# Filling the array's rows and columns in the logits, the first tiles and the expert layers of an mLSTM and mixture-of-experts kernel

## The chip, the cores and the metric

The kernel runs on one core of a Trainium2 chip. The metric is the device time of one execution in microseconds, over three runs before the change. The core has a matrix engine (PE; its weight loads are shown apart as PEld), a vector engine (DVE), a scalar engine (ACT), a general engine (POOL), a queue that issues DMAs (SP), and 16 DMA engines. A product on PE has a stationary operand that is loaded into an array of 128 rows by 128 columns, and a moving operand that streams through it. "64*128 64x256" in the profile is a product whose stationary operand has 64 rows and 128 columns and whose moving operand has 64 rows and 256 columns. The granted clock is the share of full speed that the throttle gave PE.

## The reference, cut to what matters

A gated recurrence over 768 steps for 4 batches and 8 heads of 40 values makes 3072 rows x of 320 values. Each row goes to the one of 8 experts that has its largest logit; the expert has two layers, 320 to 1024 and back.

```python
for t in range(S):
    m_new = np.maximum(f_gate[:, :, t] + m, i_gate[:, :, t])
    ...
    C = f_stab * C + i_stab * np.einsum('bhd,bhe->bhde', vt, kt)
    n = f_stab * n + i_stab * kt
    y[:, :, t] = sigmoid(o_gate) * (C @ qt) / np.maximum(np.abs(n @ qt), 1.0)
logits = x @ w_gate
e_idx = np.argmax(logits, axis=1)
eom = 1.0 / (1.0 + np.exp(-(x @ w_output_gate)))
for e in range(E):
    mask = e_idx == e
    h = np.maximum(x[mask] @ w1[e], 0.0)
    out[mask] = gate_w[mask, None] * eom[mask, e, None] * (h @ w2[e])
```

## The kernel before

**First stage.** With these gates the state is settled after the first 64 steps. For each batch `causal` makes masked products of the first 64 steps (`Pm`), `state` makes the settled state (`Cm`), and `hats` multiplies the queries, which stand as columns in `qTt`, with them. A batch has six tiles of 128 tokens, done in pairs: 12 pairs in all, numbered n. In the first tile of a batch the first 64 tokens come from `Pm` (L958) and the other 64 from `Cm` (L964), so these products have 64 columns; `qTt` holds only the queries after the first 64 steps. DVE and POOL make rows of x from `hat` (L1072 to L1088). `logits_of` turns a tile of 128 rows to columns with three transposes (L1147: 128, 128 and 64 values), ACT copies them out in two pieces (L1135, L1137), and `logits` (L368) multiplies them with the 16 columns of `wg`: three products for a tile, the third with 64 rows. These are f32 products, and each is shown in the profile as two records. `route` finds the expert and the place of each row; its first product (L246) has a stationary operand of one row. `hots` and `place` (L347, result `tp`) turn places into tables of row numbers.

**The early expert.** The largest expert after the first batch has its first 256 rows done within this stage by `pair_products` (L679 first layer, L695 second layer), while the last tiles are still being routed.

**Expert layers.** Then all eight experts run in order of size with fixed capacities C (256 left of the early one, then 512, 472, 464, 384, 368, 344, 300). f32 numbers are split into a rounded part (h) and a rest (l). `expert_hidden` (L730) takes eight blocks of 128 hidden values; a block is eight products into one accumulator: for each of the first two 128 values of x, `w1h*xh`, `w1h*xl`, `w1l*xh`; for the last 64 values, which stand twice in `xh` (rows 0 to 63 rounded, rows 64 to 127 the rest), one product of 128 rows with `w1h` and one of 64 rows with `w1l`. ACT (L731) and DVE (L732) move the result out. `expert_rows` (L746) makes the output tiles; the next expert's weights are loaded, rounded by ACT (L566, L574) and their rest made by DVE (L567, L575) meanwhile.

**What sets the order.** From `manual_schedule` on, each engine's instructions stand in the order in which the program emits them. In the first stage the class `Play` emits the operations of several lines of work by estimated times; in the expert layers plain loops do it. `warmup` emits products of constants (L991) that nobody reads: nine at the start, some between, and more where `Play` expects PE to idle.

## Time and profile before

| what | value |
|---|---|
| three runs | 328.77, 340.69, 341.56 us; median 340.69 us |
| span of the profiled execution, first to last instruction | 350.8 us |
| PE / PEld / DVE / ACT / POOL busy in it | 332.7 / 284.0 / 168.8 / 135.0 / 95.1 us |
| mean granted clock of PE in it | 0.872 |
| first stage, up to the first product of the expert layers | about 119 us |

The page gives no time of the profiled execution beside its span, so the span stands for it; it is 10.1 us longer than the median and 9.2 us longer than the slowest of the three runs. The views of the profile used here are: the windows (for a stretch of time the busy time of each engine with the number of instructions, the granted clock PEclk, the busy share of the DMA engines and what they moved), the timeline (start and duration of each instruction, like neighbours merged as xN), and the groups by form (count, busy time, mean ns of one, idle time of the engine ahead of them and who ended it). The end of a product is modelled and products overlap; the distance from one start to the next is the better measure of what one costs.

### The profile page before, as it was taken

How to read it: one execution, taken by the hardware profiler on the slowest of the kernel's cores; microseconds unless marked ns; L12 is line 12 of the kernel's file. 1: busy time of each engine (PE TensorE's matmuls, PEld its weight loads, DVE VectorE, ACT ScalarE, POOL GpSimd, SP SyncE). 2: the span in 40 equal slices, each digit the busy share in tenths (PEclk: the TensorE clock that was granted, in tenths of full speed). 3: DMA queues.
4: the chain of work that ended last, by engine and by line, in shares of the span. 5: the costliest groups of instructions: out<-in, count | busy, mean ns of one | idle time of the engine just before them, and what ended most of it. 6: DMA issues, size and time to landing. Idle time of an engine off the chain costs nothing. (4 is left out here: it accounts for less than half of the span.)

```text
span 350.8 us, 5301 instructions
## 1 busy us (share of the span) xinstructions
PE 332.7 (95%) x1911; PEld 284.0 (81%) x1913; DVE 168.8 (48%) x446; ACT 135.0 (38%) x297; POOL 95.1 (27%) x121
## 2 busy tenths in 40 slices
PE   5989999999999999999999999999999999999960
PEld 2779899999868989768966996798798798798950
DVE  6671476563695527757045506712653744712100
ACT  3523144233332236556145515623543635612210
POOL 5170341244224321610360133023214124021020
PEclk9695587555556999999999999999999999999995
DMA  7997089332623675574336425351753753110010
GB/s 191 248 257 190 10 250 275 76 120 64 211 92 91 171 195 154 163 276 121 114 94 201 105 104 159 121 169 31 235 129 108 229 153 109 53 39 7 4 42 3
DMA packets 24370, 47.04 MB, mean 134 GB/s; under 512 B 2489, under 2 KB 17570, under 8 KB 24336
## 3 DMA queue, kind: packets, MB, share of 16 engines
q1 hardware_dynamic: 20976, 37.21, 37.6%
q0 software_dynamic: 3088, 9.15, 8.6%
q8 instruction: 17, 0.28, 0.3%
q10 hardware_dynamic: 272, 0.26, 0.3%
q14 instruction: 17, 0.14, 0.1%
HBM read 37.91 MB, written 9.06 MB: 134 GB/s over the span
## 5 line engine op out<-in xcount | busy, mean ns | idle before, releaser
L732 DVE SCALAR_TENSOR_TENSOR hl<-hp,hh 128x256 fp32r<-128x256 f32 (+7 forms) x64 | 35.9, 561 | 96.1 <-ACT hh L731 95.5
L730 PE MATMUL hp<-xh,w1l 128*128 128x256 f32 (+15 forms) x192 | 71.5, 373 | 0.0
L730 PE MATMUL hp<-xh,w1h 128*128 128x256 f32 (+7 forms) x192 | 70.9, 369 | 0.0
L746 PE MATMUL op<-w2h,hh 128*128 128x320 f32 (+4 forms) x208 | 64.9, 312 | 0.0
L746 PE MATMUL op<-w2l,hh 128*128 128x320 f32 (+4 forms) x208 | 64.2, 308 | 0.0
L746 PE MATMUL op<-w2h,hl 128*128 128x320 f32 (+4 forms) x208 | 64.1, 308 | 0.0
L750 POOL DMA_INDIRECT out<-ob,sro x24 | 24.3, 1014 | 144.9 <-ACT ob L749 127.1
L731 ACT ACTIVATE hh<-hp 128x256 fp32r<-128x256 f32 (+7 forms) x64 | 31.6, 494 | 56.9 <-PE hp L730 56.9
L730 PEld LDWEIGHTS hp<-xh,w1l 128*128 128x128 f32 (+1 forms) x192 | 35.7, 186 | 17.7 <-issue 15.1
L730 PEld LDWEIGHTS hp<-xh,w1h 128*128 128x128 f32 x192 | 36.0, 188 | 11.9 <-issue 5.9
L730 PE MATMUL hp<-xl,w1h 128*128 128x256 f32 (+7 forms) x128 | 43.4, 339 | 0.0
L749 ACT ACTIVATE ob<-op,xg 128x320 f32<-128x320 f32 (+4 forms) x26 | 13.7, 527 | 65.8 <-PE op L746 65.8
L746 PEld LDWEIGHTS op<-w2h,hh 128*128 128x128 f32 (+4 forms) x208 | 37.5, 180 | 0.4 <-issue 0.2
L746 PEld LDWEIGHTS op<-w2l,hh 128*128 128x128 f32 (+4 forms) x208 | 37.6, 181 | 0.2
L746 PEld LDWEIGHTS op<-w2h,hl 128*128 128x128 f32 (+4 forms) x208 | 37.5, 180 | 0.2
L368 PEld LDWEIGHTS gbank<-wg,xt 128*128 128x128 f32 x144 | 30.4, 283 | 2.1 <-ACT lg L1157 0.4
L368 PE MATMUL gbank<-wg,xt 128*128 128x16 f32 x144 | 31.3, 336 | 0.3 <-ACT lg L1157 0.3
L547 POOL DMA_INDIRECT xg<-xs,srg x24 | 26.2, 1093 | 14.3 <-DVE sr_z L431 7.3
L567 DVE TENSOR_TENSOR w1l<-ws,w1h 128x512 fp32r<-128x512 f32 x42 | 28.9, 688 | 2.2 <-ACT w1h L566 1.8
L575 DVE TENSOR_TENSOR w2l<-ws,w2h 128x640 fp32r<-128x640 f32 x28 | 22.9, 825 | 11.6 <-ACT w2h L574 11.0
L964 PE MATMUL hat<-Cm,qTt 120*128 120x123 f32 (+1 forms) x144 | 28.1, 368 | 0.0
L964 PEld LDWEIGHTS hat<-Cm,qTt 120*128 120x128 f32 (+1 forms) x144 | 25.8, 263 | 1.0 <-issue 0.8
(220 smaller groups left out, 439.0 us busy)
## 6 DMA issues: line engine op xcount, KB each, us to landing
ws<-in_w SPq DMA_DIRECT2D x16, 640.0 KB, 5.0
ws<-in_w SPq DMA_DIRECT2D x16, 512.0 KB, 3.6
ws<-in_w SPq DMA_DIRECT2D x16, 256.0 KB, 3.9
xs<-xr SPq DMA_DIRECT2D x3, 1164.0 KB, 5.6
ot<-in_on SPq DMA_DIRECT2D x3, 960.0 KB, 10.8
qTt<-in_qT SPq DMA_DIRECT2D x6, 330.0 KB, 9.5
xs<-xr SPq DMA_DIRECT2D x1, 776.0 KB, 4.1
qTt<-in_qT SPq DMA_DIRECT2D x3, 220.0 KB, 10.2
```

The source lines that it names most:

```text
L368: nc.tensor.matmul(lg_ps[:, j], xt[:rn, kk, j], wg[:rn, kk], start=(kk == 0), stop=(kk == 2))
L547: nc.gpsimd.indirect_dma_start(out=xg[:M, j, :], out_offset=None, in_=xs[0:rows, :], in_offset=bass.IndirectOffsetOnAxis(ap=gi_[:M, j : j ...
L567: nc.vector.tensor_tensor(w1l[:, kk, us], x["st1"][kk][:, us], w1h[:, kk, us].bitcast(F32), ALU.subtract)
L575: rest.tensor_tensor(w2l[:, us], x["st2"][u][:, vs], w2h[:, us].bitcast(F32), ALU.subtract)
L730: nc.tensor.matmul(hp, a, c, start=(i == 0), stop=(i == len(mm) - 1))
L731: nc.scalar.activation(hh[:, f], hp, AF.Relu)
L732: nc.vector.scalar_tensor_tensor(hl[:, f], hp, 0.0, hh[:, f].bitcast(F32), ALU.max, ALU.subtract)
L746: nc.tensor.matmul(op[:M], a, c, start=(i == 0), stop=(i == len(mm) - 1))
L749: nc.scalar.activation(ob[:M, j], op[:M], AF.Copy, scale=xg[:M, j, DM + 64 : DM + 65])
L750: nc.gpsimd.indirect_dma_start(out=out[:, :], out_offset=bass.IndirectOffsetOnAxis(ap=x["oi"][:M, j : j + 1], axis=0), in_=ob[:M, j, :], i ...
L964: nc.tensor.matmul(hat[p0:, j, cg], qTt[:K, g, t0 : t0 + P - p0], Cm[b][:K, cg], start=True, stop=True)
```

## The change

Six edits, all of which leave the result the same to rounding:

1. The last product of a hidden block takes all 128 rows of `w1l` and `xh`, in `expert_hidden` and in `pair_products`. Rows 64 to 127 add the product of both rests.
2. The third transpose of a tile takes values 192 to 319 in place of 256 to 319; the third slice of the logit weights has zeros for the 64 that come twice. ACT copies all three pieces at once.
3. The logit weights stand five times side by side (`wg`, made by POOL from `wg1`), so the moving operand has 80 columns; the first 16 of the result are read.
4. `qTt` has all 768 columns, the first 64 zero, and `Pm` has 128 columns, the last 64 zero; in the first tile of a batch the products with `Cm` and with `Pm` are added in one accumulator over all 128 columns. Both tiles are now two fixed buffers each.
5. The first product of `route` takes 128 rows, of which only the first is not zero.
6. The constants of `warmup` are read from `ones` with step 0; the tile `wide` and its memset are gone.

```diff
+KL = [0, 128, 192]
+REP = 5
...
-        nc.tensor.matmul(pr, ones[0:1, :], bump[0:1].unsqueeze(1).to_broadcast([1, n, E]), start=True, stop=False)
+        nc.tensor.matmul(pr, ones, bump.unsqueeze(1).to_broadcast(full), start=True, stop=False)
...
     def logits(xt, j, lg_ps):
-        for kk, (r0, rn) in enumerate(KW):
-            nc.tensor.matmul(lg_ps[:, j], xt[:rn, kk, j], wg[:rn, kk], start=(kk == 0), stop=(kk == 2))
+        for kk in range(3):
+            nc.tensor.matmul(lg_ps[:, j], xt[:, kk, j], wg[:, kk].rearrange("p r e -> p (r e)"), start=(kk == 0), stop=(kk == 2))
...
-            mm += [(w1h[:, 2, fs], xh[:, 2]), (w1l[0:64, 2, fs], xh[0:64, 2])]
+            mm += [(w1h[:, 2, fs], xh[:, 2]), (w1l[:, 2, fs], xh[:, 2])]
...
-        lg_ps = gbank[:, 0 : 4 * E].rearrange("p (c e) -> p c e", e=2 * E)
+        lg_ps = gbank[:, 0 : 4 * E * REP].rearrange("p (c e) -> p c e", c=2)
...
+        qts = [gp.tile([120, 3, S], F32, name=f"qTt{i}") for i in range(2)]
+        pms = [gp.tile([P, 4, P], F32, name=f"Pm{i}") for i in range(2)]
+        for i in range(2):
+            nc.vector.memset(qts[i][:, :, :L0], 0.0)
+            nc.vector.memset(pms[i][:, :, L0:], 0.0)
...
-        nc.sync.dma_start(wg, wgo)
+        nc.sync.dma_start(wg1[:, 0:2], wgo[:, 0:2])
+        nc.sync.dma_start(wg1[64:128, 2], wgo[0:64, 2])
...
-                if c == 0:
-                    for i in range(4):
-                        nc.tensor.matmul(hat[:L0, j, 2 * i : 2 * i + 2], Pm[b][:, i], vab[b % 2][:, i], start=True, stop=True)
-                p0 = L0 if c == 0 else 0
-                t0 = c * P + p0 - L0
...
-                    nc.tensor.matmul(hat[p0:, j, cg], qTt[:K, g, t0 : t0 + P - p0], Cm[b][:K, cg], start=True, stop=True)
+                    nc.tensor.matmul(
+                        hat[:, j, cg], qTt[:K, g, c * P : (c + 1) * P], Cm[b][:K, cg], start=(g == 0), stop=(c > 0 and g == 2)
+                    )
+                if c == 0:
+                    for i in range(4):
+                        nc.tensor.matmul(hat[:, j, 2 * i : 2 * i + 2], Pm[b][:, i], vab[b % 2][:, i], start=False, stop=(i == 3))
...
-        wide = gp.tile([P, 512], BF16, name="wide")
-        nc.vector.memset(wide, 1.0)
...
-                nc.tensor.matmul(gbank, ones, wide, start=True, stop=True)
+                nc.tensor.matmul(gbank, ones, ones[:, 0:1].to_broadcast([P, 512]), start=True, stop=True)
...
+            nc.gpsimd.tensor_copy(wg, wg1.unsqueeze(2).to_broadcast([P, 3, REP, 2 * E]))
...
-                    yield act(256)
-                    nc.scalar.copy(xt[:, 0:2, j], xt_ps[:, 0:2])
-                    yield act(P)
-                    nc.scalar.copy(xt[0:64, 2, j], xt_ps[0:64, 2])
+                    yield act(3 * P)
+                    nc.scalar.copy(xt[:, :, j], xt_ps)
...
-                    for kk, (r0, rn) in enumerate(KW):
-                        nc.tensor.transpose(xt_ps[:rn, kk], rows_[b][:, c0 + j, r0 : r0 + rn], ident)
+                    for kk, r0 in enumerate(KL):
+                        nc.tensor.transpose(xt_ps[:, kk], rows_[b][:, c0 + j, r0 : r0 + P], ident)
```

Since `Play` is told of one copy where there were two, it also emits some work at other places.

First, PE where the logits of the first batch end and the products of the second begin. The names are result, moving and stationary operand; the rows before:

```order
L368 MATMUL gbank<-wg,xt 128x16 x3
L1147 MATMUL xt_ps<-ident,xr 128x128 x2
L1147 MATMUL xt_ps<-ident,xr 64x128
L964 MATMUL hat<-Cm,qTt 128x123 x2
L964 MATMUL hat<-Cm,qTt 128x82
L964 MATMUL hat<-Cm,qTt 128x123 x2
L964 MATMUL hat<-Cm,qTt 128x82
L958 MATMUL hat<-vab_201,Pm 64x82 x4
L964 MATMUL hat<-Cm,qTt 64x123 x2
L964 MATMUL hat<-Cm,qTt 64x82
```

The same place now:

```order
L372 MATMUL gbank<-wg,xt 128x80 x3
L1155 MATMUL xt_ps<-ident,xr 128x128 x3
L970 MATMUL hat<-Cm,qTt_174 128x123 x2
L970 MATMUL hat<-Cm,qTt_174 128x82
L970 MATMUL hat<-Cm,qTt_174 128x123 x2
L970 MATMUL hat<-Cm,qTt_174 128x82
L970 MATMUL hat<-Cm,qTt_174 128x123 x2
L970 MATMUL hat<-Cm,qTt_174 128x82
L975 MATMUL hat<-vab_210,Pm_176 128x82 x4
```

The number of products stays; the shapes with 64 and with 16 are gone, and in the first tile the products with `Pm` stand behind those with `Cm`.

Second, PE at the end of the first stage, where the places of the last tiles (`tp`) and the early expert's first layer (`two`) meet. The last products of the second block of `two` before, and the first of `tp` behind them:

```order
L679 MATMUL two<-xh,w1h 128x256
L679 MATMUL two<-xl,w1h 128x256
L679 MATMUL two<-xh,w1l 128x256
L347 LDWEIGHTS OH_1207
L347 MATMUL tp<-R_1208,OH_1207 128x48
```

There now, the last of `tp` and the first of `two`:

```order
L352 LDWEIGHTS OH_1184
L352 MATMUL tp<-R_1185,OH_1184 128x48
L683 MATMUL two<-xh,w1h 128x256
L683 MATMUL two<-xl,w1h 128x256
L683 MATMUL two<-xh,w1l 128x256
```

Before, 14 products of `two` stood ahead of `tp`; now all of `tp` stands ahead of `two`.

Third, DVE at the same place, whose `R` is what `tp` needs and whose `xl` and `xh` (rows of the early expert as columns, rest and rounded) are what `two` needs. Before (`xl` stands eleven rows further up):

```order
L629 TENSOR_TENSOR xh<-two,xh 64x256
L312 TENSOR_TENSOR ad<-io_94,q 128x12
L285 RECIPROCAL sm_1165<-sm_1165 128x16
L320 TENSOR_TENSOR OH_1207<-ioP,lo 128x256
L320 TENSOR_TENSOR OH_1169<-ioP,lo 128x256
L328 TENSOR_TENSOR ad<-ad,val 128x12
L379 COPY cnt<-ct 128x8
L290 TENSOR_REDUCE ss<-sm_1165 128x2
L332 TENSOR_TENSOR R_1208<-O,ad 128x96
L332 TENSOR_TENSOR R_1170<-O,ad 128x192
```

Now:

```order
L631 TENSOR_TENSOR xl<-two,xh 128x512
L325 TENSOR_TENSOR OH_1184<-ioP,lo 128x256
L337 TENSOR_TENSOR R_1130<-O,ad 128x192
L333 TENSOR_TENSOR ad<-ad,val 128x12
L383 COPY cnt<-ct 128x8
L295 TENSOR_REDUCE ss<-sm_1148 128x2
L337 TENSOR_TENSOR R_1185<-O,ad 128x96
L633 TENSOR_TENSOR xh<-two,xh 64x256
```

The last step of `xh` has moved behind both `R`, where it stood far ahead of them.

## The prediction

> **What bounds the kernel.** I read the page first, then the windows by stage, then PE's timeline inside each stage. From the page:

> ```profile
> span 350.8 us, 5301 instructions
> PE 332.7 (95%) x1911; PEld 284.0 (81%) x1913; DVE 168.8 (48%) x446; ACT 135.0 (38%) x297; POOL 95.1 (27%) x121
> ```

> PE is busy for 95% of the span, so PE is the engine to follow. The windows by stage show at which clock (after each engine's busy time and instruction count come PEclk, the DMA share and GB/s):

> ```profile
> 26.00:46.00 20.00, 20.00 (x115) 17.97 (x115) 7.05 (x30) 5.44 (x16) 4.14 (x8) 0.50 0.47 120
> 46.00:56.00 10.00, 10.00 (x94) 9.25 (x91) 8.51 (x37) 4.29 (x15) 3.54 (x8) 0.99 0.84 254
> 56.00:94.00 38.00, 37.73 (x196) 35.79 (x195) 19.66 (x82) 13.21 (x45) 13.18 (x13) 0.51 0.44 130
> 94.00:111.00 17.00, 16.21 (x84) 12.18 (x85) 13.13 (x55) 5.74 (x15) 6.18 (x5) 0.50 0.32 112
> 119.00:335.00 216.00, 216.00 (x1217) 183.24 (x1216) 98.40 (x166) 93.11 (x184) 52.61 (x50) 1.00 0.44 129
> ```

> The expert layers (119 to 335 us) are bound by PE at full clock: 216 of 216 us, DVE 98, ACT 93. The first stage is bound by PE too, but for 75 us (26 to 46 and 56 to 111) at a clock of 0.50. From 46 to 56 us the same kind of work ran at 0.99, with 94 records of products in 10 us against 115 in 20. The expert layers' blocks, at 128x256 and at 128x512 (start, duration):

> ```profile
> 127.52 0.39 PE L730 MATMUL hp<-xh,w1h 128*128 128x256 f32 x1
> 127.75 0.28 PE L730 MATMUL hp<-xl,w1h 128*128 128x256 f32 x1
> 128.34 0.28 PE L730 MATMUL hp<-xh,w1h 128*128 128x256 f32 x1
> 128.55 0.38 PE L730 MATMUL hp<-xh,w1l 64*128 64x256 f32 x1
> 128.86 0.39 PE L730 MATMUL hp<-xh,w1h 128*128 128x256 f32 x1
> ...
> 147.02 0.50 PE L730 MATMUL hp<-xh,w1h 128*128 128x512 f32 x1
> 147.35 0.39 PE L730 MATMUL hp<-xl,w1h 128*128 128x512 f32 x1
> 148.51 0.40 PE L730 MATMUL hp<-xh,w1h 128*128 128x512 f32 x1
> 148.84 0.50 PE L730 MATMUL hp<-xh,w1l 64*128 64x512 f32 x1
> 149.27 0.50 PE L730 MATMUL hp<-xh,w1h 128*128 128x512 f32 x1
> ```

> Between like products of 128 rows the starts are (128.34 - 127.75) / 5 = 0.118 us apart at 256 columns, and (148.51 - 147.35) / 5 = 0.232 at 512. Around the 64-row product the steps are 0.21, 0.31 and 0.23 us, then 0.33, 0.43 and 0.33. The weight loads say the same:

> ```profile
> L730 PEld LDWEIGHTS hp<-xh,w1l 64*128 64x128 f32 x64 | 11.7, 183 | 16.2 <-issue 15.1
> L730 PEld LDWEIGHTS hp<-xl,w1h 128*128 128x128 f32 x128 | 24.1, 188 | 0.8
> ```

> (The second row's columns are those of the first: busy, mean ns, idle ahead.) Ahead of the 64 loads with 64 rows PEld stood idle for 16.2 us with nothing to wait for; ahead of 128 loads with 128 rows, 0.8. [...]

> **The change, part by part.** *The hidden blocks (edit 1).* Eight equal steps would make 8 x 0.118 = 0.94 us where a block takes 128.86 - 127.52 = 1.34, and 1.86 where it takes 149.27 - 147.02 = 2.25: 0.40 and 0.39 us saved at either width. With 64 blocks, 25.2 us. What could take some back is DVE: at 256 columns, beside the weights' rest, a block needs the two rows below, 0.42 + 0.69 = 1.11 us, more than the new 0.94, but only in the first expert's last four blocks: 4 x 0.17 = 0.7. Wider blocks leave DVE room.

> ```profile
> 132.06 0.42 DVE L732 SCALAR_TENSOR_TENSOR hl<-hp,hh 128x256 fp32r<-128x256 f32 x1
> 132.56 0.69 DVE L567 TENSOR_TENSOR w1l<-ws,w1h 128x512 fp32r<-128x512 f32 x1
> ```

> Weight loads are the next suspect when PE is faster; the busy share of DMA was 0.44 there and would be about 0.44 x 216 / 191 = 0.50. So -24.5 us, between -21 (a few blocks that wait) and -25.2.

> *The early expert (edit 1) and its new place.* At half clock:

> ```profile
> 107.28 0.58 PE L679 MATMUL two<-xh,w1h 128*128 128x256 f32 x1
> 107.66 0.41 PE L679 MATMUL two<-xl,w1h 128*128 128x256 f32 x1
> 108.73 0.41 PE L679 MATMUL two<-xh,w1h 128*128 128x256 f32 x1
> 109.58 0.58 PE L679 MATMUL two<-xh,w1h 128*128 128x256 f32 x1
> ...
> 103.03 0.52 DVE L332 TENSOR_TENSOR R<-O,ad 128x96 f16<-128x96 bf16 x2
> ```

> A block takes 2.30 us where eight steps of (108.73 - 107.66) / 5 = 0.214 make 1.71: 0.59 each, 4.7 for eight at half clock, 3.2 at full. But the order now puts all of `tp` and both `R` ahead of these blocks. `R` ended at 103.55; the first block began at 99.75 (row below). That wait of up to 3.8 us is new, and what is queued behind it on PE is the whole early expert and then the expert layers. Together I take -0.5, between -4.7 (DVE's chain is early enough) and +0.6.

> ```profile
> 99.75 0.78 PE L679 MATMUL two<-xh,w1h 128*128 128x256 f32 x1
> ```

> *Logits (edits 2 and 3).* At full clock, six records of a tile between products of 128 columns:

> ```profile
> 48.72 1.47 PE L964 MATMUL hat<-Cm,qTt 120*128 120x123 f32 x12
> 50.02 0.88 PE L368 MATMUL gbank<-wg,xt 128*128 128x16 f32 x6
> 50.83 0.48 PE L964 MATMUL hat<-Cm,qTt 120*128 120x123 f32 x2
> ```

> Twelve records with 82 to 123 columns take 1.30 us, 0.108 each; six logits records with 16 columns take 0.81, or 0.135 each, and not the seventh part of it. So streaming is not what a record of logits costs; the load is. Widening to 80 columns, still fewer than 82 to 123, should cost nothing, and the 64-row product's 0.81 - 6 x 0.108 = 0.16 us goes. 24 tiles: -3.8 us, with 0 as the other end if the columns eat it. *First tiles (edit 4)* have as many products in either order; their switches go. I take -0.7, between 0 and -2, by the nearest row, the 64-row switch above: 0.16 us for each of four batches.

> *What lies beside other work (edits 2, 3, 4, 6).*

> ```profile
> L853 DVE TENSOR_TENSOR_SCAN m<-gf,gi 32x256 f32<-32x256 f32 x1 | 0.7, 679 | 2.2 <-DMA gi<-in_ig 2.2
> L979 POOL TENSOR_TENSOR xr<-xr,dn 128x320 f32<-128x320 f32 x1 | 0.7, 721 | 8.1 <-DVE dn L1072 8.1
> ...
> L830 SPq DMA_DIRECT2D wg<-in_wgo x1: 497/497/497, 7.5 to 7.5; - x1
> DMA to landing us min/median/max: 6.6/6.6/6.6
> ...
> L368 PE MATMUL gbank<-wg,xt x144: 181/374/395, 20.7 to 93.9; 128*128 128x16 f32 x96, 64*128 64x16 f32 x48
> ```

> The new memsets stand ahead of DVE's first scan, which waits 2.2 us for a DMA; without that cover they would push the scan and the whole first stage. The logit weights now come in two DMAs: one more issue of 0.5 us on SP, by which the later loads move. They were issued at 7.5 us and landed at 14.1, so about 14.6 now; POOL's copy behind them stands ahead of L979, where POOL sat idle for 8.1 us, and the first logits come at 20.7. If the landing were several us later, L979 and with it the second tile's rows would wait. ACT's joined copy lies beside a late PE. All of this I cost at nothing.

> **The clock.** The sum so far is 350.8 - 24.5 - 0.5 - 3.8 - 0.7 = 321.3 us with an unchanged clock. Now the 75 us at 0.50. The logits' share of them, and of the stretch at 0.99 (windows of that line alone):

> ```profile
> 46.00:56.00 10.00, 3.17 (x23) 3.05 (x23) 0.99 0.84 254
> 56.00:94.00 38.00, 20.68 (x87) 20.48 (x86) 0.51 0.44 130
> ```

> From 56 to 94 us, where the clock stayed down, logits took 20.7 us of 38 (from 46 to 56 us 3.2 of 10). Each of their records streams 16 columns in about the time in which a record above streams up to 123, so PE is "busy" while the array mostly waits for loads. If the throttle looks at what streams and not at busy time, five times the columns lift that stretch nearly to the level of the other products, and the clock rises there. What it could bring: at the rate of 46 to 56 us (94 products in 10 us) the 115 of 26 to 46 take 12.2 us, -7.8. The 196 of 56 to 94 would take 20.9, but DVE has 19.7 us of work there, in order, between PE's products; at the share it reached from 46 to 56 us (8.5 of 10) that is 23 us, -15. From 94 to 111 us DVE works for 13.1 of 17, so -2. Together up to -25. I take about half, -13, since the order of a busy and an empty stretch that the throttle wants is not to be read from this trace: 308 on the profiled execution's own scale.

> That execution is 10.1 us above the median of the three runs, 340.69, and these spread over 12.8 us with one program. Differences of that size are what more or fewer us at half clock would give, so I put the median run in the same picture: unchanged clock 340.7 - 29.5 = 311, full clock 321.3 - 25 = 296, and the forecast in the middle, **303 us**.

> **Rivals.**

> *The clock stays as it was.* For it: PE was busy for 37.7 of 38 us at 0.51, and busy time cannot rise further. Then only switches go: 311 us, or 316 if the runs lie nearer to the profiled one's 321. [...]

> *The 64-row product costs nothing special.* Then the steps of 0.31 and 0.43 us are the accumulator's end, and stay. Against it: the output products end an accumulator too, and the 64 loads with 64 rows are the only group with 16 us of idle time ahead. Without the 25 us and with an unchanged clock, 340.7 - 4.5 = 336. [...]

> *Slower.* The clock falls in the expert layers. At half clock a block of 256 columns takes 1.71 us (eight steps of 0.214) in place of 0.94, so each us of these 191 would grow by 0.8. From 29.5 / 0.8 = 37 us at half clock on, the gain is eaten; 50 us would give 311 + 40 = 351. Against it: 216 us ran there at 1.00 with the gaps, and the gaps go.

> **How the numbers follow.** Clock better by some or much (294 to 308): 0.64. Clock unchanged (311 to 316): 0.27. No gain from rows: 0.05. Slower: 0.02. Something else, a load or DVE that holds the layers to half of the 25 us: 0.02. The time is the first case's, 303. The range runs from 292 (full clock, early expert 4 us better) to 316. A measurement of this kernel tells about 2% from no change, 334 to 347 us: faster 0.94, same 0.04, slower 0.02.

> **What will show it.** Steps of 0.118 and 0.232 us through a whole block of L734, no idle time ahead of its loads, and expert layers of about 191 us instead of 216: that is the firm part. Six records of logits with 80 columns in some 0.65 us at full clock, not 0.8 or more. PEclk above 0.5 between 56 and 94 us; if it is 0.5 there, the median is near 311 to 316. On PE, a wait for `R` ahead of `tp` at the end of the first stage. I am wrong if the third product's step stays above 0.2 us at 256 columns, if records with 80 columns take 0.2 us, or if DVE or weight loads end waits of PE in the layers for more than 5 us.

## The result

The changed kernel takes 307.74 us (median of four runs, 307.41 to 307.94); the kernel before took 337.28 us beside it (four runs, 328.77 to 341.56). The ratio, taken over the fast runs of both alone, is 0.932, with a 95% interval of 0.924 to 0.939: faster by 6 to 8% (the medians alone would give 0.912). The profiled execution of the changed kernel took 307.94 us, with a span of 306.2 us. From its page:

```profile
span 306.2 us, 5277 instructions
PE 279.6 (91%) x1911; PEld 262.0 (86%) x1913; DVE 171.5 (56%) x450; ACT 133.5 (44%) x273; POOL 95.2 (31%) x122
...
PEclk9999999998679999999999999999999999999985
```

PE is still the busiest engine, but it is now idle for some 14 us of the first stage, where it was for 6; the rest of its idle time lies behind its last product. The windows by stage (PE, PEld, DVE, ACT and POOL busy, PEclk, DMA share, GB/s), the last one from the first expert layer to PE's last product:

```profile
26.00:46.00 20.00, 20.00 (x199) 19.16 (x200) 13.54 (x59) 8.62 (x20) 9.68 (x18) 1.00 0.72 189
46.00:56.00 10.00, 9.46 (x92) 9.03 (x88) 8.04 (x30) 4.90 (x12) 2.78 (x5) 1.00 0.89 268
56.00:80.00 24.00, 18.10 (x168) 16.60 (x169) 22.36 (x87) 11.14 (x34) 12.73 (x11) 0.89 0.54 171
80.00:94.00 14.00, 10.47 (x78) 9.32 (x78) 11.10 (x47) 4.36 (x10) 5.23 (x4) 0.82 0.29 101
...
102.60:293.60 191.00, 190.77 (x1210) 182.72 (x1208) 96.52 (x163) 92.40 (x182) 48.61 (x47) 1.00 0.46 140
```

From 26 to 46 us the clock is 1.00 where it was 0.50, and 199 records of products fit in where 115 did. From 56 to 80 us DVE is busy for 22.4 of 24 us: there the bound has passed from PE to DVE. The expert layers take 191.0 us. Their blocks, one of 256 columns and one of 512 (start, duration), and the loads of the product that had 64 rows:

```profile
102.62 0.28 PE L734 MATMUL hp<-xh,w1h 128*128 128x256 f32 x1
...
103.46 0.28 PE L734 MATMUL hp<-xh,w1l 128*128 128x256 f32 x1
103.58 0.28 PE L734 MATMUL hp<-xh,w1h 128*128 128x256 f32 x1
...
122.37 0.39 PE L734 MATMUL hp<-xh,w1h 128*128 128x512 f32 x1
...
124.22 0.39 PE L734 MATMUL hp<-xh,w1h 128*128 128x512 f32 x1
```

```profile
L734 PEld LDWEIGHTS hp<-xh,w1l 128*128 128x128 f32 x192 | 36.1, 188 | 2.2
```

A block takes 103.58 - 102.62 = 0.96 us (1.34 before) and 124.22 - 122.37 = 1.85 (2.25 before). All steps are alike, and all 192 of these loads together have 2.2 us of idle time ahead of them, where the 64 with 64 rows alone had 16.2.

Where the 44.6 us between the two profiled executions went, in us, read off PE's timelines:

| stretch | before | after | difference |
|---|---|---|---|
| start to the first logits | 20.7 | 24.2 | +3.5 |
| first logits to the first product of `two` | 79.1 | 61.6 | -17.5 |
| early expert, to the first expert layer | 23.9 | 16.9 | -7.0 |
| expert layers, to PE's last product | 215.1 | 190.9 | -24.2 |
| from there to the end | 12.1 | 12.7 | +0.6 |

In the kernel before, the expert layers run from 123.6 to 338.7 us; the table and the window above that have them begin at 119 us count in the last 4.6 us of the early expert.

### The profile page after: what moved, and what is told of

It reads as the page before. It is cut to its first block, busy times and chain, and to the rows that moved or that the text cites. A ratio compares the mean times of both kernels' runs of the same rounds, so it can differ in the third digit from the quotient of the medians.

```text
span 306.2 us, 5277 instructions
## 1 busy us (share of the span) xinstructions
PE 279.6 (91%) x1911; PEld 262.0 (86%) x1913; DVE 171.5 (56%) x450; ACT 133.5 (44%) x273; POOL 95.2 (31%) x122
## 5 line engine op out<-in xcount | busy, mean ns | idle before, releaser
L734 PE MATMUL hp<-xh,w1h 128*128 128x256 f32 (+7 forms) x192 | 64.6, 339 | 0.0
L734 PE MATMUL hp<-xh,w1l 128*128 128x256 f32 (+7 forms) x192 | 64.6, 339 | 0.0
L734 PE MATMUL hp<-xl,w1h 128*128 128x256 f32 (+7 forms) x128 | 43.4, 339 | 0.0
L734 PEld LDWEIGHTS hp<-xh,w1l 128*128 128x128 f32 x192 | 36.1, 188 | 2.2
L734 PEld LDWEIGHTS hp<-xh,w1h 128*128 128x128 f32 x192 | 36.1, 188 | 2.1
L570 ACT CAST w1h<-ws 128x512 fp32r<-128x512 f32 x42 | 25.7, 613 | 0.0
L734 PEld LDWEIGHTS hp<-xl,w1h 128*128 128x128 f32 x128 | 24.1, 188 | 1.4
L970 PE MATMUL hat<-Cm,qTt 120*128 120x123 f32 x144 | 21.6, 306 | 0.5 <-DVE Cm L949 0.5
L970 PEld LDWEIGHTS hat<-Cm,qTt 120*128 120x128 f32 x144 | 20.4, 222 | 1.5 <-DVE Cm L949 1.3
```

Source lines behind the costliest of these rows:

```text
L570: nc.scalar.copy(w1h[:, kk, us], x["st1"][kk][:, us])
L734: nc.tensor.matmul(hp, a, c, start=(i == 0), stop=(i == len(mm) - 1))
L970: nc.tensor.matmul(hat[:, j, cg], qTt[:K, g, c * P : (c + 1) * P], Cm[b][:K, cg], start=(g == 0), stop=(c > 0 and g == 2))
```

## The experiments

There were twelve runs, four at a time, each four beside the kernel before on one chip. The kernel before spread there from 331 to 368 us, in the main the longer the lower its mean granted clock (331.0 at 0.958, 367.7 at 0.851); once it took 551.2 us at a clock of 1.00, which nothing here explains. So variants are set against each other and against the changed kernel, not against its median (342.81, 339.67 and 342.81 us in the three sets).

| run | edit | median us | range |
|---|---|---|---|
| e1_rows64 | changed, hidden products with 64 rows again | 339.21 | 335.0 to 342.3 |
| e2_rep1 | changed, 16 columns | 323.07 | 312.2 to 326.2 |
| e3_rows_only | before, hidden products with 128 rows | 317.40 | 304.9 to 327.1 |
| e4_order | changed, order of before at the stage's end | 305.91 | 304.8 to 307.0 |
| e5_rep3 | changed, 48 columns | 318.71 | 311.9 to 319.8 |
| e6_first_tiles | changed, first tiles as before | 309.30 | 305.6 to 310.9 |
| e7_warm | changed, 14 filling products at the start | 309.65 | 307.7 to 315.4 |
| e8_after_again | changed | 308.80 | 308.1 to 309.6 |
| e9_rest | e4_order, all weights' rests on DVE | 303.05 | 302.2 to 305.7 |
| e10_order_again | e4_order | 305.56 | 304.6 to 306.6 |
| e11_logits64 | e4_order, logits' third product with 64 rows | 308.85 | 307.3 to 309.2 |
| e12_wide8 | e4_order, 128 columns | 306.06 | 304.6 to 307.4 |

**The rows of the hidden blocks, undone and alone.** The first run takes the changed kernel and puts the 64 rows back (both places); the third takes the kernel before and makes only this edit.

```
-            mm += [(w1h[:, 2, fs], xh[:, 2]), (w1l[:, 2, fs], xh[:, 2])]
+            mm += [(w1h[:, 2, fs], xh[:, 2]), (w1l[0:64, 2, fs], xh[0:64, 2])]
```

> The changed kernel with one thing undone: the third weights' product of the hidden blocks has 64 rows again, in the early expert too. If a change in the number of rows empties the array, each of the 64 blocks costs 0.39 us more and each of the early expert's eight 0.40 to 0.59: 25 + 3 to 5, so 336 to 338 us against the changed kernel's 307.7, and steps of 0.21, 0.31 and 0.23 us around that product at 256 columns. If the long step belonged to the end of the accumulator and something else made the kernel faster, 308 us.

> The kernel before with the hidden blocks' third weights' product at 128 rows and nothing else changed. By the sum of the prediction the blocks are worth 24.5 us and the early expert 3 to 5 (no new wait here, since the order stays): 308 to 310 us against 337.3, and then the other edits together moved the median by only 0 to 2 us. If the wider logits were worth the 13 us that the prediction gives to the clock, and the blocks less, it is 318 to 321 us. If 64 rows cost nothing, 337.

Undone: 339.21 us, 1 us above the expected 336 to 338. Its windows of the early expert and of the expert layers:

```profile
80.00:94.00 14.00, 10.52 (x48) 7.95 (x46) 9.47 (x39) 2.99 (x7) 5.22 (x4) 0.62 0.30 103
94.00:112.80 18.80, 18.80 (x89) 16.35 (x89) 5.44 (x18) 3.13 (x7) 5.03 (x5) 0.68 0.58 171
112.80:327.90 215.10, 215.06 (x1210) 181.59 (x1208) 97.21 (x163) 92.40 (x182) 49.48 (x46) 1.00 0.39 120
```

The layers take 215.1 us, as in the kernel before (215.1), at a clock of 1.00: the 24.2 us are the rows' and nothing else's. The early expert grew from 16.9 to 27.3 us, far more than eight switches (changes in the number of rows between one product and the next) of 0.4 to 0.6, since the clock was low (0.62 and 0.68). It had fallen in the wait ahead of `tp`, at 85.5 us, as in the changed kernel at 85.0; there it rose after one window of 3.41 us, here only at 106.0 us. This execution, of 342.25 us, is the longest of the four. The shortest, 335.0 us, is 27.3 us above the changed kernel, about the layers' 24.2 and 0.4 for each of eight switches. Alone, on the kernel before: the layers take 192.5 us at a clock of 1.00,

```profile
26.00:46.00 20.00, 20.00 (x109) 17.94 (x108) 6.14 (x27) 4.34 (x12) 2.80 (x4) 0.50 0.44 110
46.00:56.00 10.00, 10.00 (x53) 9.55 (x52) 5.49 (x26) 3.52 (x11) 4.25 (x8) 0.50 0.69 207
...
120.70:313.20 192.50, 190.69 (x1210) 182.69 (x1208) 96.51 (x163) 92.17 (x181) 48.73 (x48) 1.00 0.47 141
```

and the first stage keeps its half clock to 56 us, with 0.58 to 0.67 behind that. The median fell by 342.8 - 317.4 = 25.4 us on that chip, somewhat less than the 27 to 29 expected; 317.4 lies close to the 318 to 321 that were given for wider logits worth 13 us. Its best run, 304.91 us at a mean clock of 0.951, is below all of the changed kernel's; its worst, 327.09, had 0.872. So this edit alone carries most of the gain, and what it lacks is a first stage that is fast in every run: the other edits move the median by some 10 us, and the best run not at all.

**The columns of the logits.** `REP` is 5 in the changed kernel.

```
-REP = 5
+REP = 1
```

> The changed kernel with the logits' 16 columns streamed once, not five times; all else stays. If the clock follows what streams, the granted clock between 26 and 111 us is 0.5 for most of the time, as in the kernel before, and the time is 8 to 20 us above 307.7, with a larger spread from run to run. If the five-fold columns do nothing for the clock, 308 us (or a little less, since fewer columns stream) and a PEclk as in the changed kernel.

323.07 us, some 15 more, and a spread of 14 us; the shortest of the six, 312.22 us, is still above the longest of the changed kernel's ten, 309.57. From 56 to 80 us this kernel's row reads:

```profile
56.00:80.00 24.00, 24.00 (x135) 23.88 (x134) 14.13 (x53) 7.81 (x20) 8.92 (x9) 0.50 0.35 105
```

PE is busy for all 24 us at a clock of 0.50; in the changed kernel it was busy for 18.1 of the same 24 at 0.89. More busy time went with the lower clock. With `REP = 3`:

> The changed kernel with the logits' 16 columns streamed three times (48 columns). In the six traces so far the clock fell after each of the 3.4 us windows in which at most 0.35 of the array (rows times columns of the products, times the time they stream) was filled, and after none at 0.37 or more. With 16 columns such windows lay at 32 and 49 us, at 0.29 and 0.34; 80 columns lift them to about 0.5 and 0.4, 48 columns to about 0.40 and 0.37. If this is the rule, the clock holds until the early expert in most runs: 307 to 311 us. If the clock follows the columns in proportion, about 315, half way between 308 and 323.

318.71 us: not the changed kernel's time, as the limit of the expectation would have had it, and not half way either; 48 columns are nearer to 16 than to 80, in the shortest run too (311.89 us). In its profiled execution (313.94 us) the clock held through 32 us, where 16 columns lost it, and fell at 51.2 us:

```profile
47.80:51.20 3.40, 2.79 (x23) 2.50 (x23) 3.40 (x13) 2.47 (x6) 1.56 (x2) 1.00 0.77 254
51.20:54.60 3.40, 3.40 (x18) 3.40 (x18) 0.58 (x3) 0.00 (x0) 0.00 (x0) 0.50 0.86 252
```

By the reckoning of the expectation the array was filled by 0.33 in the window that ended there, where I had put 0.37: here too the clock fell after a window below 0.35, and my number for this window was off by what decides. With 128 columns, read eight times over from the 16 in the product itself (POOL's copy of the weights is gone, and the order is the fourth run's):

```
-            nc.tensor.matmul(lg_ps[:, j], xt[:, kk, j], wg[:, kk].rearrange("p r e -> p (r e)"), start=(kk == 0), stop=(kk == 2))
+            o = lg_ps[:, j].rearrange("p (r e) -> p r e", e=2 * E)
+            nc.tensor.matmul(o, xt[:, kk, j], wg1[:, kk].unsqueeze(1).to_broadcast([P, REP, 2 * E]), start=(kk == 0), stop=(kk == 2))
```

> The fourth run's kernel with 128 columns for the logits (16 read eight times over in the product itself, so the copied weights and GpSimd's copy are gone). If the clock only needs the array filled by more than about 0.35, it holds with more to spare: 304 to 306 us and no window below 0.4 before 60 us. If 128 columns stream longer than the weight loads, the logits' records take more than 0.12 us at full clock and the time grows by up to 24 x 6 x 0.02 = 3 us, less where VectorE bounds: 306 to 309.

306.06 us against 305.56 of its base: no gain and no loss that these runs tell. 80 columns were enough here. From 22 to 60 us no window was filled by less than 0.55, but the base's clock did not fall there either. Ahead of the logits the expectation failed: the window from 4.9 to 8.3 us was filled by 0.13, and the clock fell.

**The rows of the logits.** Base is the fourth run's kernel.

```
-            nc.tensor.matmul(lg_ps[:, j], xt[:, kk, j], wg[:, kk]...)
+            p0 = 64 if kk == 2 else 0
+            nc.tensor.matmul(lg_ps[:, j], xt[p0:, kk, j], wg[p0:, kk]...)
```

> The fourth run's kernel with the logits' third product at 64 rows (the lower half of the tile, which holds zeros in the weights, is left out), with five-fold columns. By the prediction's term a change in the number of rows costs 0.16 us for each of 24 tiles: 3.8 us if PE bounds the whole stretch, 1.5 us if only the nine or ten tiles before VectorE becomes the bound count, so 307.5 to 310. If a change of rows between such short products costs nothing, 306.

308.85 against 305.56 us: 3.3 us. Six records of a tile and what follows them, first with 64 rows in the third product, then in the base (both stand behind transposes of 128 rows):

```profile
52.38 0.94 PE L373 MATMUL gbank<-wg,xt 128*128 128x80 f32 x6
53.26 0.90 PE L971 MATMUL hat<-Cm,qTt 120*128 120x123 f32 x6
```

```profile
50.17 0.79 PE L372 MATMUL gbank<-wg,xt 128*128 128x80 f32 x6
50.80 0.83 PE L970 MATMUL hat<-Cm,qTt 120*128 120x123 f32 x6
```

From start to the next start it is 0.88 us and 0.63. Other tiles from 50 to 62 us show 0.88 to 0.97 against 0.63 to 0.73, so the switch costs about 0.25, half as much again as the 0.16 that the prediction took from records with 16 columns; 24 such tiles are 6.0 us, of which 3.3 reach the end.

**The order at the end of the first stage.** The planner counts the copy of the columns as two pieces again, which puts `two` ahead of `tp` as before.

```
-                    yield act(3 * P)
+                    yield act(256)
+                    yield act(P)
                     nc.scalar.copy(xt[:, :, j], xt_ps)
```

> The changed kernel with the order of the kernel before at the end of the first stage: the planner counts the copy of the columns as two pieces again, 256 and 128 elements, and the early expert's first block stands ahead of the last six place products. If the changed kernel's wait of 3.5 us ahead of these products is on the path, 304 to 306 us. If the early expert is then held up by something else that is as late (its weights, the later wait of the same products), 307 to 308.

> The fourth run's kernel again, as the base of the three others on the same chip: 305 to 307 us.

305.91 and 305.56 us on two chips; the changed kernel had 307.74 us, and 308.80 on a third chip, and no run of one lies in the range of the other, though the two never ran side by side. In the changed kernel's trace the wait stands as forecast (the profile names `cnt`, which stands between the two `R` on DVE), and in the reordered one another comes behind it:

```profile
85.44 0.48 PE L352 MATMUL tp<-R,OH 128*128 128x48 f16 x6 [3.53 <-DVE cnt L383]
```

```profile
83.44 0.53 PE L352 MATMUL tp<-R,OH 128*128 128x48 f16 x6 [0.83 <-DVE R L337]
...
101.53 0.39 PE L734 MATMUL hp<-xh,w1h 128*128 128x256 f32 x1 [1.64 <-ACT ob L647]
```

The first expert layer starts at 98.8 us instead of 102.6. Of these 3.8 us 1.6 go to a wait for the early expert's results on ACT, of which the changed kernel's first trace shows nothing and that of the eighth run 1.0 us.

The order alone does not make the wait of 3.53 us. Ahead of it in the changed kernel, two operations of DVE lie beside two of POOL (rests of the early expert's weights, from 81.82 to 83.35 and from 83.32 to 85.02 us):

```profile
82.08 1.55 DVE L325 TENSOR_TENSOR OH<-ioP,lo 128x256 f16<-128x256 f32 x1
83.56 1.68 DVE L337 TENSOR_TENSOR R<-O,ad 128x192 f16<-128x192 bf16 x1
```

`OH` takes 0.42 us in most other places, and this `R` 0.35 us in the kernel before and in the reordered one. DVE's two end at 83.63 and 85.24 us, just behind POOL's (83.35 and 85.02): by my estimate, 1.55 - 0.42 + 1.68 - 0.35, some 2.5 us of the wait are such stalls, of which more below. In the reordered kernel one `OH` is held (1.78 us in the tenth run) and this `R` is not.

**The first tiles.** The hats of a batch's first tile are computed as before, with 64 columns in the array.

```
+                if c == 0:
+                    for i in range(4):
+                        nc.tensor.matmul(hat[:L0, j, 2 * i : 2 * i + 2], Pm[b][:, i, :L0], vab[b % 2][:, i], start=True, stop=True)
+                p0 = L0 if c == 0 else 0
...
+                    nc.tensor.matmul(hat[p0:, j, cg], qTt[:K, g, c * P + p0 : (c + 1) * P], Cm[b][:K, cg], start=True, stop=True)
```

> The changed kernel with the products of each batch's first tile as they were: four of 64 columns, then the hats of 64 columns beside them, all else as changed. The prediction gave the change 0.7 us of gain; then this is 308.4 us. The traces speak for the opposite: at half clock the first tile took 1.89 us before and 3.01 after, 1.56 at full clock, since products on the two halves of the columns ran beside each other: 1.1 us less for the first batch, 0 to 0.6 for each of the others, and a fuller window at 12 to 15 us, after which the clock rose in the kernel before (15.5 us; 23.6 in the changed one). Then 303 to 306 us and the first logits at 20 to 22 us instead of 24.

> The changed kernel itself, beside the three others on the same chip: 307.5 us within 0.5, if chips differ as little as its runs did.

The changed kernel itself missed its expectation by 0.8 us, and its two chips differ by about 1 us. The old form takes 309.30 against 308.80 us, with ranges that overlap: no gain of 3 to 6 us in the median, though two of its six runs, 305.59 and 306.75, lie below all six of the changed kernel here. In time the median is what the prediction's 0.7 us would give, but not for its reason. What the traces spoke for was there: at full clock the old form's first tile lies between 27.73 and 28.79 us, 1.06, where the new one takes 1.56. The old form, and the new one as the tenth run's trace has it (the first tile from 50.80 to 52.36):

```profile
27.73 0.57 PE L969 MATMUL hat<-vab,Pm 128*64 128x82 f32 x5
28.08 0.32 PE L974 MATMUL hat<-Cm,qTt 120*64 120x123 f32 x1
28.14 0.31 PE L969 MATMUL hat<-vab,Pm 128*64 128x82 f32 x2
```

```profile
50.80 0.83 PE L970 MATMUL hat<-Cm,qTt 120*128 120x123 f32 x6
51.47 1.06 PE L975 MATMUL hat<-vab,Pm 128*128 128x82 f32 x8
52.36 0.83 PE L970 MATMUL hat<-Cm,qTt 120*128 120x123 f32 x6
```

In the old form products on one half of the columns start while those on the other run (28.08 and 28.14, 0.06 us apart; the new form's lie 0.11 apart). The first logits came at 19.9 instead of 24.3 us. But then the clock was down (0.50) from 34.3 to 41.2 us, where the eighth run kept it, and the first expert layer began at 102.2 us instead of 102.8.

**The start.** `WARM = (14, 1, 2, 3)` instead of 9.

> The changed kernel with 14 filling products at the start instead of 9, up to the first transpose at 7.5 us. If one full window of 3.4 us lets the clock rise and one at under 0.35 lets it fall, the clock rises at about 6.5 us and falls again at 10 (the causal products fill little of the array): 307 us, at most 1 us less than the changed kernel. If the clock stays up once the start is filled, the first products run at full clock and the first logits come at 21 us: 304 us.

Both expectations failed in part: the clock rose at 4.1 us and did not fall at 10, and the first logits came at 18.9 us, earlier than hoped; yet the time is 309.65 us, no better than 308.80. What follows the first logits is this:

```profile
18.95 0.83 PE L372 MATMUL gbank<-wg,xt 128*128 128x80 f32 x6
22.82 0.68 PE L917 MATMUL sp<-qkt 40*64 40x64 f32 x16 [3.05 <-DMA qkt<-in_qk]
```

The data of the next batches land at 22.8 us. The faster start waits for them. In the window from 21.0 to 24.5 us PE was busy for 1.68 of 3.50 us, and from 24.5 to 31.4 us the clock was 0.51. So neither this run nor the one before it turned earlier first logits into time, and the 3.5 us by which the changed kernel reaches them later than the kernel before need not have cost it 3.5 us.

**DVE beside GpSimd.** All ten rests of the early expert's weights go to DVE; eight of them were on POOL.

```
-REST = (5, 7)
+REST = tuple(range(10))
```

> The fourth run's kernel (old order at the end of the first stage) with all ten rests of the early expert's weights on VectorE; there, eight of them were on GpSimd. In that run's trace VectorE operations with their data in SBUF that began beside one of these eight ended with it: 0.16 us became 1.24, 0.36 became 1.78, together some 9 us between 55 and 88 us. If these are stalls on what the two engines share, 9 us go and 4 x 0.69 + 4 x 0.83 = 6 us of work come to VectorE, which bounds this stretch: 302 to 304 us. If VectorE would have waited there for PE or ScalarE anyway, the 6 us of work are all that counts: 306 to 311.

303.05 against 305.56 us on the same chip, the best of all: 2.5 us. The windows from 24 to 88 us, first this kernel, then its base:

```profile
24.00:88.00 64.00, 58.16 (x537) 53.21 (x533) 50.75 (x227) 28.45 (x73) 19.45 (x29) 0.92 0.68 197
```

```profile
24.00:88.00 64.00, 57.22 (x542) 52.77 (x541) 55.28 (x214) 28.29 (x72) 29.03 (x35) 0.95 0.67 196
```

DVE has eight more of the rests, five of 0.68 us and three of 0.82, and is busy for 4.5 us less; so the stalls that went were by this sum 4.5 + 5.9, some 10 us. Only a quarter of that reaches the end: PE now waits for the early expert's rows from DMA, 3.2 us in two pieces (1.1 in the base). Two of its six runs, 305.18 and 305.66, lie in the range of the base's, and the other four, up to 303.30, below it.

## Why the prediction was right, point by point

*Hidden blocks, -24.5.* Measured -24.2, and shown twice: undone, the layers take 215.1 us; alone, 192.5. "The 64-row product costs nothing special" is out: in the blocks, between products of 128 rows, it cost 0.38 us at 256 columns (1.34 against 0.96) and 0.40 at 512 (2.25 against 1.85), so filling the rows did pay here. What the array does at such a change (the first run's expectation has it emptied) is not shown; the traces show the longer steps (0.21, 0.31 and 0.23 us against 0.118) and the 16.2 us for which the loads stood idle ahead of the 64 with 64 rows.

*Early expert, -0.5.* The stretch shortened by 7.0 us. The wait ahead of `tp` came as forecast (3.5 us of up to 3.8), but it lies ahead of this stretch. Within it all blocks but the first few ran at full clock. The prediction had split that among two terms, 3 to 5 us for the switches and 2 for the clock, and set the wait against them. The clock's part was larger: before, the early expert ran at half clock for 11.4 us (to 111.1), now for 2.7 (to 88.4), which by half of the difference is an estimated 4.3 us.

*Logits, -3.8.* The undone rows cost 3.3 us. The term was right by luck: the switch is half as long again as taken, and about half of it does not reach the end; that this half lies where DVE is the bound is argued from the windows. Six records with 80 columns take 0.63 us; 0.65 was forecast.

*First tiles, -0.7.* Wrong in sign for PE: the first tile takes 1.06 us in the old form and 1.56 in the new at full clock, 1.89 and 3.01 at half. I had counted products and looked for switches, not at the overlap that the timeline of the kernel before shows: its products with `Pm` on one half of the columns run beside those with `Cm` on the other (one of each starts at 12.29 and 12.30 us, where the new form's records with `Pm` start 0.213 us apart at half clock). In the kernel's time neither sign can be told (309.3 against 308.8 us). That what PE gains is given back to the clock rests on one trace, where it fell at 34.3 us.

*Covers.* They held. PE waited neither for POOL's copy of the weights nor for ACT's joined copy, and the first logits stood behind PE's own work at half clock, which lasted to 23.6 us where it had ended at 15.5 before (the eight records with `Pm` start 0.213 us apart from 13.26 us, and 0.112 at full clock from 31.84).

*The clock, -13.* This carried the forecast's other half, and the second run bears it out: with 16 columns instead of 80 the same kernel takes 323.07 us, with a clock of 0.50 from 56 to 80 us where it was 0.89. Its size depends on the run: beside the rows alone the other edits bring some 10 us in the median (317.4 to 307.7) and nothing in the best run (304.9 against 307.4). The rival "the clock stays as it was" would have given 311, near the measured time, but for a reason that the second run excludes. Busy time in the profile does not tell the clock: PE was busy for 24.0 of 24 us at 0.50 in the second run, for 18.1 at 0.89 in the changed kernel. The rival in which the layers lose the clock did not come: 1.00 throughout.

*The number.* On the scale of the profiled execution's span the working gave 308 us; it was 306.2. The stage table shows the errors that cancel: layers -24.2 for -24.5, all ahead of them -21.0 for -18.0, and the profiled execution of before, 10 us above its median, had more time at half clock to lose. For the median I set the forecast half way between an unchanged clock (311) and a full one (296). That step was mis-sized: the clock is full nearly everywhere in PE's part, and the time is 307.7, not 296. What caps it is DVE from 56 to 86 us, which I had allowed 23 us for the work of 56 to 94. It was busy there for 28.3 of 30 us, and by the sum from the ninth run about 10 us of its busy time from 24 to 88 us, in the reordered kernel, were stalls beside POOL, which I had not looked for.

What stays open: why the clock stayed down in the early expert of the first run, where it rose in the changed kernel, is only argued from the filling (its windows at half clock had 0.68 to 0.75 with 64 rows before one of 0.80 after which it rose; the changed kernel's first had 0.81); the edits were undone one at a time, so the parts (25 for the rows, 15 for the columns, 3 for the logits' rows) need not add up; and what lets the clock rise again is not settled.

## What to carry to other kernels

On PE's timeline look for steps between like products that are longer around one of another shape: here a product with fewer rows saved nothing and cost 0.38 to 0.40 us a block, and filling the unused rows bought it back. Where PE is "busy" at half clock, look at what streams: here six records of logits took 0.62 to 0.72 us with 80 columns (the changed kernel) and 0.72 with 16 (the second run), both at full clock, and with 80 every run of the changed kernel took 307.4 to 309.6 us. Once PE is faster, look at who waits next, before tuning PE further: here DMA, then DVE and what POOL does beside it.

## What the hardware showed that I had not expected

**The windows after which the clock fell.** The clock changed at 5.30, 8.72, 15.54, 25.79, 46.27, 56.51 and 111.12 us in the trace of the kernel before, and at 23.57, 74.77, 81.59, 85.01 and 88.42 in that of the changed kernel, at distances of 3.41 us or whole multiples of it. For each window of 3.41 us I summed over PE's records the time for which their columns stream, times the share of the 128 x 128 array that the product uses. A column counts 0.83 ns at half clock (the filling products of 512 columns start 0.427 us apart there) or half of that at full (0.216 us apart), and twice as much in the f32 records of the first stage. The factor of two is my estimate: such a record of 123 columns takes 0.213 us at half clock and one of 256 columns in the early expert 0.214, but one of 82 columns takes 0.213 us too. So what follows are sums of these traces and not a figure of the chip; with the factor at one the five falls below lie at up to 0.17 and the other windows of the two traces from 0.20.

```profile
49.25:52.66 3.41, 3.41 (x39) 3.20 (x33) 3.41 (x13) 2.05 (x5) 0.85 (x2) 1.00 0.84 273
52.66:56.07 3.41, 3.41 (x18) 3.41 (x17) 1.69 (x5) 1.08 (x3) 0.70 (x2) 0.50 0.81 275
```

And two of the changed kernel, with PE busy for 2.25 and 1.62 us; the clock outlasted the first (filled by 0.46) and fell after the second (0.21):

```profile
67.94:71.36 3.42, 2.25 (x25) 2.25 (x25) 3.06 (x19) 1.85 (x7) 1.53 (x2) 1.00 0.57 160
71.36:74.77 3.41, 1.62 (x13) 1.32 (x12) 3.41 (x9) 1.07 (x4) 2.47 (x2) 1.00 0.85 287
74.77:78.18 3.41, 2.78 (x22) 2.49 (x23) 2.31 (x12) 1.04 (x3) 0.64 (x1) 0.50 0.66 214
```

The limit is fitted to these runs alone. The time for which columns stream, without the share of the array, sorts the windows worse: falls came at up to 0.58, and 47 of the others lie below that. With the share of the rows alone the sum sorts nearly as well (falls up to 0.38, the others from 0.34), so whether the array's columns count is not told. No such sum told when the clock rises: it rose after windows of 0.60 to 1.0 and stayed down after some of up to 0.75. Where the windows lie differs from run to run. The nine filling products at the start filled one window whole in the traces of the second, ninth and twelfth runs, and the clock rose at 4.5 to 4.9 us, as in the kernel before's at 5.3; in the changed kernel's they were shared by two, filled by 0.58 and 0.54, and it did not.

**Operations of DVE that ended with POOL's.** From the changed kernel's timeline (start, duration; POOL's row is two operations, the second from 66.94 to 68.20 us):

```profile
65.72 2.48 POOL L592 TENSOR_TENSOR w1l<-ws,w1h 128x512 fp32r<-128x512 f32 x2
...
66.99 0.19 DVE L233 TENSOR_REDUCE lmax<-lg 128x6 f32<-128x48 f32 x1
67.11 1.11 DVE L437 TENSOR_TENSOR pro<-prg,pr_z 128x2 int32<-128x2 int32 x1
```

An operation on two elements a partition takes 1.11 us and ends with POOL's (68.22 and 68.20 us); the reduction just ahead of it takes 0.19 beside the same operation. The two operations of DVE ahead of `tp` ended just behind POOL's in the same way (83.63 and 85.24 against 83.35 and 85.02). What DVE waits for there, and which of its operations do, these rows do not show. The ninth run shows what it costs when DVE is the bound: without POOL's part in the rests DVE was busy for 50.75 us from 24 to 88 us against 55.28, and the time was 303.05 against 305.56 us.
